# F1 of batch 0 kept in SBUF, with one f32 matmul a step, and its loads for F2 as two DMAs of four rows each

## The chip, the cores and the metric

The kernel runs on one core of one Trainium2 chip. The metric is the time of one execution on the device, in microseconds (us). Each kernel was timed in several runs; the profile is of one further execution. TensorE is called PE below, VectorE DVE, ScalarE ACT, GpSimd POOL, and SyncE, which issues all DMAs of this kernel, SP.

## What is computed

A spectral layer over 8 sequences (batches) of 3008 rows and 256 columns, and an MLP over all of its rows, in float32:

```python
X = np.fft.rfft(x, axis=1)
Yr = Xr @ w_r - Xi @ w_i + b_r
Yi = Xr @ w_i + Xi @ w_r + b_i
Yr = np.sign(Yr) * np.maximum(np.abs(Yr) - lam, 0.0)
Yi = np.sign(Yi) * np.maximum(np.abs(Yi) - lam, 0.0)
y = np.fft.irfft(Y, n=x.shape[1], axis=1)

h = y @ w_in
g = h - np.tanh(h)
return (g @ w_out).astype(np.float32)
```

w_in (256 x 2048) and w_out (2048 x 256) arrive as float64 and are taken apart on the chip into a high and a low float32 part.

## The kernel before

3008 = 64 x 47, and the Fourier transform is made in two factors. **F1** is the transform of length 47, over the rows of x; of its output 24 frequencies are needed, and real and imaginary parts of two of the 64 residues (a *pair*; there are 32) give 96 rows. **F2** is the transform of length 64, over the pairs. Each batch runs F1 (8 chunks of 4 pairs, class Forward), F2 with the linear layer and the shrinking (12 *units* of two frequencies each, class Spectrum), the inverse of F2 (still a unit; its result z goes to DRAM), and the inverse of F1 (class Unit, which reads z back). The MLP then takes chunks of 512 rows.

Between F1 and F2 the axis that lies on the partitions changes: F1 leaves 96 rows (parity, real or imaginary, frequency) by pair and column, and F2 needs 128 rows (parity, real or imaginary, pair) for one frequency. Before, batch 0 made that exchange in DRAM as the others do: `keep` copied a step's result from PSUM to a tile `st` and wrote it to `a_dram` (`a<-st`), and `load` of a unit read two frequencies back into the tile `at` (`at<-a`, one DMA of 256 KB).

All five engines run in an order that is written out by hand (`manual_schedule`), and each engine works through its own list in that order. Batch 0 stands at the start of the program:

- Loads on SP, in this order: the table of F1, the eight chunks `xt` of x, the table of F2. SP has one DMA queue.
- 11 matmuls on no data (`idle`) while the first loads come in.
- F1: 16 steps, two to a chunk. A step splits x into a high float32r part (a cast on ACT) and the rest (a subtraction on DVE), makes three matmuls of 512 columns (lines 235 to 237) and one idle matmul; two steps later `keep` (line 249) copies the result, on ACT or DVE. The loads of w_r, w_i, the biases and the table i1 are issued between the later steps.
- 16 idle matmuls.
- F2: in round i of a loop SP issues the load of unit i + 2, PE makes the transform of unit i (line 339), the products of unit i - 1 with the linear layer's weights (lines 442 and 448, which take the copies `xf` and the sum `sf` of the transform), and the inverse of unit i - 3 (line 471). The tile `at` has three buffers, so the load of unit i + 2 waits for the transform of unit i - 1. `combine_linear` (lines 125 to 139) and the split of i1 prepare the tables that the products and inverses need. Between these steps ACT and DVE take apart the first of the 16 pieces of w_in and w_out (`w_raw`, 512 KB each, loaded on the same queue; `some`).

In this stage F2 uses f32 matmuls, which the trace records as two matmuls each; an instruction's count in the trace is then twice that of the program.

Of the kernel before, what the change touches and what calls it, by code (L numbers as in the profile page):

```python
# [10 lines left out]
F32 = mybir.dt.float32  # L11
F32R = mybir.dt.float32r
# [5 lines left out]
NP, NJ = 32, 24  # L18
# [16 lines left out]
def dft_constants():  # L35
# [14 lines left out]
    di = np.stack([-s, c], 2).transpose(1, 0, 2, 3).reshape(128, 128)  # L50
    f2 = np.concatenate([dr[:, :96], dr[:, 32:], di[:, :96], -di[:, 32:]], 1)
    ph = 2 * np.pi * np.outer(np.arange(64), n1) / 64
    sg = np.where(np.arange(64) < 32, 1.0, -1.0)[:, None]
# [17 lines left out]
    i2 = i2.transpose(1, 0, 2).reshape(128, -1)  # L71
    return [np.ascontiguousarray(v, np.float32) for v in (f1, f1s, f2, i1, i2)]


@with_exitstack
def spectral_ffn(ctx, tc, x, w_r, w_i, b_r, b_i, w_in, w_out, x_twice, f1, f1s, f2, i1, i2, out):
    nc = tc.nc
# [62 lines left out]

    win_h = const.tile([P, 2, FF], F32R, name="win_h")
    win_l = const.tile([P, 2, FF], F32R, name="win_l")
    wout_h = const.tile([P, NF, D], F32R, name="wout_h")
    wout_l = const.tile([P, NF, D], F32R, name="wout_l")

# [26 lines left out]
    def split_f64(part, k, raw):  # L172
        if k < 2:
            sl = slice(part * WB, (part + 1) * WB)
            hi_out, lo_out = win_h[:, k, sl], win_l[:, k, sl]
        else:
            n = WB // D
            f = part * WB // P + (k - 2) * n
            hi_out, lo_out = (w[:, f:f + n].rearrange("p t e -> p (t e)") for w in (wout_h, wout_l))
        top, low = raw[:, :, 1], raw[:, :, 0]  # L180
# [28 lines left out]
    class Forward:  # L209
# [4 lines left out]
        def load(self):  # L214
            if self.ch == 0:
# [6 lines left out]
            nc.sync.dma_start(out=self.xt, in_=x[:, self.b * NP + self.ch * XC:self.b * NP + (self.ch + 1) * XC, :])  # L222
# [8 lines left out]
        def dft(self, q):  # L231
            xh, xl = self.x[q]
            self.ps[q] = bank("ps_f1")
            pv = self.ps[q][:96].rearrange("p (a d) -> p a d", d=D)
            nc.tensor.matmul(pv, f1l, xh, start=True, stop=False)
            nc.tensor.matmul(pv, f1h, xh, start=False, stop=False)
            nc.tensor.matmul(pv, f1h, xl, start=False, stop=True)

        def keep(self, q, copy=nc.scalar.copy):
            if self.b == 0 or self.b == 1 and self.ch >= LOOK:  # L240
                n = 2
                pool, tag, bufs = ((ffn, "th", 2), (work, "k", 5), (work, "tmp", 4))[(2 * self.ch + q) % 3] if self.b == 0 else (load, "at", 3)
                st = pool.tile([96, 2, D], F32, name="st", tag=tag, bufs=bufs)
            else:
# [67 lines left out]
    class Spectrum:  # L312
# [6 lines left out]
        def load(self):  # L319
            if self.jp == 0:  # L320
                z_dram[self.b] = dram.tile([NP, 96, D], F32, name=f"z_{self.b}", tag="z")
            self.at = load.tile([P, 2, D], F32, name="at", tag="at", bufs=3)
            nc.sync.dma_start(out=self.at.rearrange("p j d -> p (j d)"), in_=rows(a_dram[self.b][0], self.jp))
            if self.b > 2:
# [7 lines left out]
        def transform(self):  # L332
            ps = self.ps = bank("ps_f2")
            pv = ps.rearrange("p (t r j m) -> p t j r m", t=2, r=2, j=2)
            for jj in range(2):
                o = m0[2 * self.jp + jj]
                rhs = f2t.rearrange("p (r u c) -> p r u c", r=2, u=2)[:, :, :, o:o + 32]
                for t in range(2):
# [183 lines left out]
    class Chunk:  # L522
# [27 lines left out]
        def up(self, f, i):  # L550
            n = self.n
            hp = H[0][:, i % 2, :n] if H else early_h[i % 2 if i < SINGLE else 0][:, :n]
            k = 0
            for lhs, rhs in ((win_l, self.yh), (win_h, self.yh), (win_h, self.yl)):
                for t in range(2):
                    nc.tensor.matmul(hp, lhs[:, t, f * P:(f + 1) * P], rhs[:, t, :n], start=k == 0, stop=k == 5)  # L556
                    k += 1
# [10 lines left out]
        def down(self, f, gh, gl, t):  # L568
# [56 lines left out]
    class Pair:  # L625
# [13 lines left out]
        def left(self, name):  # L639
# [4 lines left out]
            t, f = {"a11": (0, 0), "a12": (1, 0), "a21": (0, 1), "a22": (1, 1)}[name]  # L644
            return [w[:, t, (2 * q + f) * P:(2 * q + f + 1) * P] for w in (win_h, win_l)]

# [51 lines left out]
    def weight_sums(p):  # L698
        wv = [w.rearrange("p k (q i m) -> p k i q m", i=2, m=P)[:, :, :, 2 * p:2 * p + 2] for w in (win_h, win_l)]
        pair = [work.tile([P, 2, 2, P], F32, name=f"ws{k}", tag="tmp", bufs=4) for k in range(2)]  # L700
# [233 lines left out]
    with tc.manual_schedule(engines={E.PE, E.Activation, E.DVE, E.Pool, E.SP}):  # L934
# [12 lines left out]
        nc.vector.memset(below, -LAM)
        f1h, f1l = split(load_whole(f1, [94, 96], "f1", tag="tmp", bufs=4), "f1", rest=nc.vector)
        first = [Forward(0, ch) for ch in range(NP // XC)]
        for f in first:  # L950
            f.load()
        f2t = load_const(f2, [P, 384], "f2")
        steps = [(f, q) for f in first for q in range(XC // 2)]
# [130 lines left out]
        for u in early_units[:3]:  # L1084
            for t in range(2):
                u.time(t)

        raw = work.tile([P, 2, 512], F32, name="raw", tag="raw", bufs=1)
        start.close()
# [149 lines left out]
```

## Time and profile before

| What | us |
|---|---|
| median of 3 runs | 2584.85 (2584.58 to 2585.59) |
| the profiled execution | 2586.71 |
| its span, from the first to the last instruction | 2584.9 |
| PE busy within the span | 2557.7 |

The profile is read in four views. The page gives busy times and shares. The chain follows the end of the program back to its start: at each step to what released it. The timeline lists instructions in order of time, with equal ones merged; the brackets at a row's end say how long the engine had stood idle and what ended it. The windows give, for a stretch of time, the busy time of each engine, the clock granted to PE as a share of the full one, and what the DMA engines did.

### The profile page before, as it was taken

The page shows a single profiled execution, that of the slowest core. Times are in us where ns is not written, and L with a number is a line of the kernel's source. Part 1 is how long each engine was busy: PE and PEld are TensorE (multiplying, and loading weights), DVE is VectorE, ACT ScalarE, POOL GpSimd, SP SyncE. Part 2 cuts the span into 40 slices and gives each one's busy share as a digit, 9 for nine tenths or more (in the row PEclk, how much of TensorE's full clock was granted, in tenths as well). Part 3 has the DMA queues.
Part 4 walks back from the last instruction along what each step waited for, and adds up shares of the span by engine and source line. Part 5 has one row for each costly group of instructions (what it writes and reads, how often), then busy time and mean ns, then how long its engine had stood idle before and what let it go on. Part 6 is the DMA issues. An engine that isn't in the chain of part 4 may idle for free.

```text
span 2584.9 us, 42892 instructions
## 1 busy us (share of the span) xinstructions
PE 2557.7 (99%) x16041; PEld 2283.9 (88%) x16041; DVE 1838.1 (71%) x2742; ACT 1608.0 (62%) x2942; POOL 792.4 (31%) x885
## 2 busy tenths in 40 slices
PE   8999999999999999999999999999999999999999
PEld 6787898899889999899999999899998999999998
DVE  6787884777777776777776777767777666666665
ACT  5556566666666666666666666666666555565655
POOL 0004334332334433333324333333333323221210
PEclk8999999999999999999999999999999999999999
DMA  6521225233333332333323342232433121111000
GB/s 192 169 84 56 89 72 152 82 99 97 95 105 118 104 116 82 98 112 107 120 72 115 97 132 90 86 116 84 131 91 95 62 73 60 47 43 47 19 27 17
DMA packets 145521, 235.87 MB, mean 91 GB/s; under 512 B 12192, under 2 KB 85152, under 8 KB 145312
## 3 DMA queue, kind: packets, MB, share of 16 engines
q1 hardware_dynamic: 145312, 233.11, 28.8%
q8 instruction: 127, 2.08, 0.3%
q14 instruction: 82, 0.67, 0.1%
HBM read 142.36 MB, written 90.70 MB: 90 GB/s over the span
## 4 chain that ended last, share of the span: by engine, by line
PE 95%; DVE 2%; DMA 1%; ACT 1%; issue 0%; POOL 0%; SPq 0%; DVEq 0%; ACTq 0%; POOLq 0%
PE o L580 39%; PE H L651 34%; PE ps_v L366 5%; PE ps_i L507 4%; PE ps_f L339 3%; PE ps_t L366 2%; PE he L556 2%; PE ps_f L285 1%; PE ps_v L448 1%; PE ps_i L413 1%; PE ps_i L415 1%; PE ps_i L414 1%; DMA a<-st 1%; PE oe L580 1%; PE ps_t L448 0%; PE ps_i L471 0%
## 5 line engine op out<-in xcount | busy, mean ns | idle before, releaser
L689 ACT CAST gh<-th 128x1024 fp32r<-128x1024 f32 x352 | 371.4, 1055 | 381.8 <-DVE th L685 253.5
L651 PEld LDWEIGHTS H<-y_t,sum 128*128 128x128 f32 x3168 | 516.2, 188 | 102.3 <-DVE th L685 5.5
L580 PE MATMUL o<-gh,wout_l 128*128 128x512 f32 x1408 | 563.2, 400 | 0.0
L580 PE MATMUL o<-gl,wout_h 128*128 128x512 f32 x1408 | 554.3, 394 | 0.5 <-DVE gl L693 0.5
L580 PE MATMUL o<-gh,wout_h 128*128 128x512 f32 x1408 | 552.7, 393 | 0.0
L651 PE MATMUL H<-y_t,sum 128*128 128x256 f32 x3168 | 545.2, 281 | 0.9 <-DVE ot L593 0.7
L693 DVE TENSOR_TENSOR gl<-th,gh 128x1024 fp32r<-128x1024 f32 x352 | 440.6, 1252 | 57.6 <-ACT gh L689 54.8
L685 DVE TENSOR_TENSOR th<-H,th 128x1024 f32<-128x1024 f32 x352 | 428.3, 1217 | 5.0 <-ACT th L682 2.3
L682 ACT ACTIVATE th<-H 128x1024 f32<-128x1024 f32 x352 | 362.6, 1030 | 42.5 <-PE H L651 42.0
L667 DVE TENSOR_TENSOR H<-H,late 128x256 f32<-128x256 f32 x352 | 152.2, 432 | 319.5 <-PE H L651 283.3
L580 PEld LDWEIGHTS o<-gl,wout_h 128*128 128x128 f32 x1408 | 264.7, 188 | 60.8 <-DVE gl L693 1.5
L673 DVE TENSOR_TENSOR H<-H,late 128x256 f32<-128x256 f32 x352 | 151.7, 431 | 191.4 <-PE H L651 183.1
L651 PE MATMUL H<-y_b,win_h 128*128 128x256 f32 x1408 | 280.8, 281 | 0.0
L580 PEld LDWEIGHTS o<-gh,wout_l 128*128 128x128 f32 x1408 | 265.0, 188 | 7.9 <-ACT gh L689 0.5
L580 PEld LDWEIGHTS o<-gh,wout_h 128*128 128x128 f32 x1408 | 264.9, 188 | 7.3
L659 ACT COPY late<-H 128x256 f32<-128x256 f32 x352 | 131.6, 374 | 211.9 <-PE H L651 209.1
L651 PE MATMUL H<-y_more,win_h 128*128 128x256 f32 x1408 | 263.1, 279 | 0.0
L97 POOL TENSOR_TENSOR z_l<-mn,z_h 128x512 fp32r<-128x512 f32 x84 | 112.5, 1340 | 431.3 <-ACT z_h L96 276.4
L651 PEld LDWEIGHTS H<-y_more,win_h 128*128 128x128 f32 x1408 | 215.3, 188 | 6.1
L651 PEld LDWEIGHTS H<-y_b,win_h 128*128 128x128 f32 x1408 | 214.4, 188 | 0.2 <-POOL y_b L97 0.2
L651 PE MATMUL H<-y_more,win_l 128*128 128x256 f32 x704 | 201.1, 286 | 1.2 <-DVE H L673 1.2
L403 DVE TENSOR_TENSOR y<-tb,ps_v 64x256 f32<-64x256 f32 x384 | 160.8, 419 | 56.8 <-PE ps_v L366 44.8
(190 smaller groups left out, 4381.3 us busy)
## 6 DMA issues: line engine op xcount, KB each, us to landing
a<-st SPq DMA_DIRECT2D x188, 192.0 KB, 3.0
x<-in_x_twice SPq DMA_DIRECT2D x55, 512.0 KB, 4.7
at<-a SPq DMA_DIRECT2D x96, 256.0 KB, 3.2
z<-zo SPq DMA_DIRECT2D x96, 256.0 KB, 2.0
zin<-z SPq DMA_DIRECT2D x64, 384.0 KB, 4.4
out<-ot SPq DMA_DIRECT2D x47, 512.0 KB, 3.1
shared<-a SPq DMA_DIRECT2D x60, 256.0 KB, 3.7
shared<-in_i SPq DMA_DIRECT2D x58, 235.0 KB, 4.0
```

Of the source, the lines that this page charges most:

```text
L97: rest.tensor_tensor(out=lo, in0=src, in1=hi.bitcast(F32), op=ALU.subtract)
L366: nc.tensor.matmul(dst, lhs[:, t], rhs[:, t, :], start=n == 0, stop=n == 5)
L403: nc.vector.tensor_tensor(out=y[ri * 64:(ri + 1) * 64, jj, :], in0=common(jj, ri), in1=self.vv[jj * 64:(jj + 1) * 64, ri * D:(ri + 1) * D] ...
L580: nc.tensor.matmul(self.o[t][:, :n], lhs[:, f, t * P:(t + 1) * P], rhs, start=f == 0 and k == 0, stop=f == NF - 1 and k == 2,)
L651: nc.tensor.matmul(dst, a, b, start=start and k == 0, stop=k == 2, skip_group_check=True)
L659: nc.scalar.copy(out=self.p7, in_=self.c11)
L667: nc.vector.tensor_tensor(out=self.c21, in0=self.acc, in1=self.p7, op=ALU.add)
L673: nc.vector.tensor_tensor(out=self.c22, in0=self.acc, in1=self.p7, op=ALU.add)
L682: nc.scalar.activation(out=self.th, in_=self.hp[:, :, :n], func=AF.Tanh)
L685: nc.vector.tensor_tensor(out=self.th, in0=self.hp[:, :, :self.n], in1=self.th, op=ALU.subtract)
L689: nc.scalar.copy(out=self.gh, in_=self.th)
L693: nc.vector.tensor_tensor(out=self.gl, in0=self.th, in1=h(self.gh), op=ALU.subtract)
```

## The change

F1 of batch 0 no longer splits x: a step is one f32 matmul on the loaded chunk. `keep` copies its result into one tile `first_a` in SBUF (96 rows; 32 KB in each), and nothing of it is written to DRAM. A unit's load is two DMAs from SBUF to SBUF, one for each of its two frequencies: each reads four rows of `first_a` (`first_a[row::NJ]`: rows `row`, `row` + 24, + 48, + 72), and spreads them, in pieces of 1 KB, over the 128 rows of `at`. The rows then come in another order, so batch 0 has its own table for F2 (`f2_first`), loaded in place of the old one; the old one is loaded after the first two units. 6 idle matmuls stand ahead of F1 instead of 11, and none between its steps. The loads for the linear layer are issued ahead of the steps.

To make room, the four tiles of the split w_in and w_out become two, for the lower and the upper half of the MLP's hidden columns; the second takes the place of `first_a` once F2 of batch 0 is over.

```diff
+    weights = [const.tile([P, 4, HF * D], F32R, name="weights0")]
+    first_a = work.tile([96, NP, D], F32, name="a_first", tag="weights1", bufs=1)
...
         def dft(self, q):
-            xh, xl = self.x[q]
             self.ps[q] = bank("ps_f1")
             pv = self.ps[q][:96].rearrange("p (a d) -> p a d", d=D)
+            if self.b == 0:
+                nc.tensor.matmul(pv, f1f, self.xt[:94, 2 * q:2 * q + 2], start=True, stop=True)
+                return
+            xh, xl = self.x[q]
...
         def keep(self, q, copy=nc.scalar.copy):
-            if self.b == 0 or self.b == 1 and self.ch >= LOOK:
+            if self.b == 0:
+                p = self.ch * XC + 2 * q
+                copy(out=first_a[:, p:p + 2], in_=self.ps[q][:96].rearrange("p (a d) -> p a d", d=D))
+                return
+            if self.b == 1 and self.ch >= LOOK:
...
             self.at = load.tile([P, 2, D], F32, name="at", tag="at", bufs=3)
+            if self.b == 0:
+                for jj in range(2):
+                    row = 2 * self.jp + jj
+                    nc.sync.dma_start(out=self.at[:, jj], in_=first_a[row::NJ])
+                return
...
-        idle(11)
+        idle(6)
...
-        for i in range(len(steps) + 2):
-            if 10 <= i < 14:
-                next(loads)
-            if i == 14:
-                i1f = load_whole(i1, [P, P], "i1", tag="s_l")
+        for _ in range(4):
+            next(loads)
+        i1f = load_whole(i1, [P, P], "i1", tag="s_l")
+        f1h, f1l = split(f1f, "f1", rest=nc.vector)
+        steps = [(f, q) for f in first for q in range(XC // 2)]
+        for i in range(len(steps) + 1):
             if i < len(steps):
-                steps[i][0].split(steps[i][1], piece(2 + i % 4, [94, 2, 2, D], F32R, "x_first"), nc.vector)
-            if 1 <= i <= len(steps):
-                steps[i - 1][0].dft(steps[i - 1][1])
-                idle(1)
-            if i >= 2:
-                f, q = steps[i - 2]
-                f.keep(q, nc.vector.tensor_copy if i % 3 == 0 else nc.scalar.copy)
+                steps[i][0].dft(steps[i][1])
+            if i >= 1:
+                f, q = steps[i - 1]
+                f.keep(q, nc.vector.tensor_copy if i % 2 == 0 else nc.scalar.copy)
...
         for u in units[:2]:
             u.load()
+        f2t = load_const(f2, [P, 384], "f2")
```

Two places show what that does to the lists. On SP, from the start of the program to the first loads for F2, before (`f_f` is F1's table, `f` F2's; `a` is the exchange in DRAM):

```order
L112 DMA f_f<-in_f 94x96
L222 DMA xt<-in_x 96x1024 x8
L107 DMA f_125<-in_f 128x384
L252 DMA a_108<-st 96x2x256 x8
L121 DMA bias<-in_b_r 128x256
...
L252 DMA a_108<-st 96x2x256 x4
L323 DMA at<-a_108 128x512 x2
L165 DMA w_raw<-in_moe_w_in 128x1024 x2
L323 DMA at<-a_108 128x512 x4
L421 DMA z_348<-zo 128x512
```

and now:

```order
L113 DMA f_f<-in_f 94x96
L229 DMA xt<-in_x 96x1024 x8
L113 DMA f_f<-in_f_first 128x384
L122 DMA bias<-in_b_r 128x256
...
L339 DMA at<-a_first 128x1x256 x4
L108 DMA f_203<-in_f 128x384
L173 DMA w_raw<-in_moe_w_in 128x1024 x2
L339 DMA at<-a_first 128x1x256 x8
L439 DMA z_196<-zo 128x512
```

The writes to DRAM are gone, each load is two, and the old table stands between the loads of unit 1 and the first two pieces of w_in.

On PE, from the start to unit 0 of F2, before (the second step's rows read as the first's, and so on to the last):

```order
L943 MATMUL idle<-warm 128x512 x11
L235 MATMUL ps_f_136<-x_first,f_l 96x512
L236 MATMUL ps_f_136<-x_first,f_h 96x512
L237 MATMUL ps_f_136<-x_first,f_h 96x512
L943 MATMUL idle<-warm 128x512
...
L943 MATMUL idle<-warm 128x512 x17
L339 MATMUL ps_f_375<-f_125,at 128x2x64 x4
```

and now:

```order
L962 MATMUL idle<-warm 128x512 x6
L242 MATMUL ps_f_128<-xt,f_f 96x512
...
L242 MATMUL ps_f_172<-xt,f_f 96x512
L962 MATMUL idle<-warm 128x512 x16
L357 MATMUL ps_f_228<-f_f,at 128x2x64 x4
```

Four matmuls a step have become one. Behind unit 0's transform PE, ACT, DVE, POOL and SP have the same operations in the same order as before, save for the doubled loads and the tiles' names.

More of the change, by code (lines that the diff above doesn't have):

```diff
@@ L51, in dft_constants @@
     f2 = np.concatenate([dr[:, :96], dr[:, 32:], di[:, :96], -di[:, 32:]], 1)
+    f2b = f2.reshape(NP, 4, 384).transpose(1, 0, 2).reshape(128, 384)
     ph = 2 * np.pi * np.outer(np.arange(64), n1) / 64
@@ L71, in dft_constants, with spectral_ffn @@
     i2 = i2.transpose(1, 0, 2).reshape(128, -1)
-    return [np.ascontiguousarray(v, np.float32) for v in (f1, f1s, f2, i1, i2)]
+    return [np.ascontiguousarray(v, np.float32) for v in (f1, f1s, f2, f2b, i1, i2)]
 @with_exitstack
-def spectral_ffn(ctx, tc, x, w_r, w_i, b_r, b_i, w_in, w_out, x_twice, f1, f1s, f2, i1, i2, out):
+def spectral_ffn(ctx, tc, x, w_r, w_i, b_r, b_i, w_in, w_out, x_twice, f1, f1s, f2, f2_first, i1, i2, out):
     nc = tc.nc
@@ L139, in combine_linear, with w_up, w_down @@
         return (wr, w2, w3), (ones, brow)
[L141 to L144, printed above, removed]
+    HF = NF // 2
+    weights = [const.tile([P, 4, HF * D], F32R, name="weights0")]
+    first_a = work.tile([96, NP, D], F32, name="a_first", tag="weights1", bufs=1)
+    def w_up(t, f, n=1):
+        lo = t * HF * P + f % HF * P
+        return [weights[f // HF][:, v, lo:lo + n * P] for v in range(2)]
+    def w_down(f, lo, n):
+        lo += f % HF * D
+        return [weights[f // HF][:, 2 + v, lo:lo + n] for v in range(2)]
     shared, turns = [], {}
@@ L173, in split_f64 @@
         if k < 2:
-            sl = slice(part * WB, (part + 1) * WB)
-            hi_out, lo_out = win_h[:, k, sl], win_l[:, k, sl]
+            hi_out, lo_out = w_up(k, part * WB // P, WB // P)
         else:
@@ L178, in split_f64 @@
             f = part * WB // P + (k - 2) * n
-            hi_out, lo_out = (w[:, f:f + n].rearrange("p t e -> p (t e)") for w in (wout_h, wout_l))
+            hi_out, lo_out = w_down(f, 0, WB)
         top, low = raw[:, :, 1], raw[:, :, 0]
@@ L214, in load @@
         def load(self):
-            if self.ch == 0:
+            if self.ch == 0 and self.b > 0:
                 a_dram[self.b] = dram.tile([2, NP, 96, D], F32, name=f"a_{self.b}", tag="a")
@@ L553, in up @@
             k = 0
-            for lhs, rhs in ((win_l, self.yh), (win_h, self.yh), (win_h, self.yl)):
+            for v, rhs in ((1, self.yh), (0, self.yh), (0, self.yl)):
                 for t in range(2):
-                    nc.tensor.matmul(hp, lhs[:, t, f * P:(f + 1) * P], rhs[:, t, :n], start=k == 0, stop=k == 5)
+                    nc.tensor.matmul(hp, w_up(t, f)[v], rhs[:, t, :n], start=k == 0, stop=k == 5)
                     k += 1
@@ L644, in left @@
             t, f = {"a11": (0, 0), "a12": (1, 0), "a21": (0, 1), "a22": (1, 1)}[name]
-            return [w[:, t, (2 * q + f) * P:(2 * q + f + 1) * P] for w in (win_h, win_l)]
+            return w_up(t, 2 * q + f)
         def product(self, dst, left, right, start=False):
@@ L698, in weight_sums @@
     def weight_sums(p):
-        wv = [w.rearrange("p k (q i m) -> p k i q m", i=2, m=P)[:, :, :, 2 * p:2 * p + 2] for w in (win_h, win_l)]
+        wv = [weights[p // 2][:, v].rearrange("p (k q i m) -> p k i q m", k=2, i=2, m=P)[:, :, :, 2 * (p % 2):2 * (p % 2) + 2] for v in range(2)]
         pair = [work.tile([P, 2, 2, P], F32, name=f"ws{k}", tag="tmp", bufs=4) for k in range(2)]
@@ L951, in spectral_ffn @@
             f.load()
-        f2t = load_const(f2, [P, 384], "f2")
-        steps = [(f, q) for f in first for q in range(XC // 2)]
+        f2b = load_whole(f2_first, [P, 384], "f2", tag="spill", bufs=1)
         loads = linear_loads()
@@ L1086, in spectral_ffn @@
                 u.time(t)
+        weights.append(work.tile([P, 4, HF * D], F32R, name="weights1", tag="weights1", bufs=1))
         raw = work.tile([P, 2, 512], F32, name="raw", tag="raw", bufs=1)
```

14 lines of the change are left out of this document (7 added, 7 removed).

## The prediction

> **What bounds the kernel now.** The page comes first: span, busy shares, and the chain of work that ended last, by engine.
>
> ```profile
> span 2584.9 us, 42892 instructions
> ...
> PE 2557.7 (99%) x16041; PEld 2283.9 (88%) x16041; DVE 1838.1 (71%) x2742; ACT 1608.0 (62%) x2942; POOL 792.4 (31%) x885
> ...
> PE 95%; DVE 2%; DMA 1%; ACT 1%; issue 0%; POOL 0%; SPq 0%; DVEq 0%; ACTq 0%; POOLq 0%
> ```
>
> TensorE (PE) ends everything: it is busy 99% of the span. What is to be had lies in the few stretches in which PE waits or works at a lower clock. The change touches only F1 and F2 of batch 0, so the second view is the chain in order of time over the first 60 us (start, length, what).
>
> ```profile
> 1.55 4.71 DMA xt<-in_x
> ...
> 7.49 8.67 DMA a<-st
> ...
> 20.55 5.22 DMA a<-st
> ...
> 26.49 3.92 DMA a<-st
> ...
> 30.55 2.72 DMA at<-a
> ...
> 33.40 3.76 PE ps_f L339 x16
> ```
>
> Until 33.40 the chain is transfers: x comes in, F1's results go out to DRAM (a<-st, three long pieces), and come back (at<-a). Only from 33.40, when F2 starts, is it PE. The third view is PE's timeline (start, length, engine, line, operation, idle time before with its releaser).
>
> ```profile
> 1.91 4.23 PE L943 MATMUL idle<-warm 128*128 128x512 f32 x11 [1.91 <-DVE below L947]
> ...
> 25.57 4.05 PE L943 MATMUL idle<-warm 128*128 128x512 f32 x17
> ...
> 33.40 3.76 PE L339 MATMUL ps_f<-f,at 128*128 128x128 f32 x16 [3.78 <-DMA at<-a]
> ...
> 42.84 1.06 PE L339 MATMUL ps_f<-f,at 128*128 128x128 f32 x8
> ...
> 46.95 1.05 PE L339 MATMUL ps_f<-f,at 128*128 128x128 f32 x8
> ...
> 51.06 1.02 PE L471 MATMUL ps_i<-mn,i_f 128*128 128x512 f32 x2
> 51.91 1.05 PE L339 MATMUL ps_f<-f,at 128*128 128x128 f32 x8
> 52.90 0.49 PE L442 MATMUL ps_v<-brow,ones 33*128 33x512 f32 x1
> ...
> 86.64 1.05 PE L339 MATMUL ps_f<-f,at 128*128 128x128 f32 x8
> ```
>
> L339 is a unit's transform in F2. Units 0 and 1 start at 33.40, unit 2 at 42.84, unit 3 at 46.95, unit 4 at 51.91, unit 11 at 86.64: from unit 3 on one unit takes (86.64 - 46.95) / 8 = 4.96 us. The last view, by windows, says who sets that, and at which clock (length, busy us of each engine, granted clock, DMA share, GB/s).
>
> ```profile
> 15.00:20.00 5.00, 2.60 (x8) 1.52 (x9) 2.60 (x5) 3.77 (x8) 0.00 (x0) 0.87 0.79 258
> 14.70:17.30 2.60, 0.00 (x0) 0.00 (x0) 0.00 (x0) 1.07 (x3) 0.00 (x0) 1.00 1.09 381
> 18.70:22.10 3.40, 3.40 (x10) 2.20 (x9) 3.04 (x5) 1.93 (x5) 0.00 (x0) 0.50 0.49 144
> ...
> 32.40:42.50 10.10, 9.10 (x28) 7.57 (x29) 2.97 (x7) 1.69 (x3) 0.00 (x0) 0.50 0.66 220
> ...
> 51.91:86.64 34.73, 34.73 (x163) 26.67 (x161) 27.47 (x59) 21.76 (x41) 0.00 (x0) 1.00 0.62 213
> ```
>
> From 51.91 to 86.64 PE is never idle at the full clock, so the 4.96 us are PE's own. From 32.40 to 42.50, after the idle 3.78 us, it runs at clock 0.50; likewise from 18.70 to 22.10, after the idle 14.70 to 17.30. The program's order after F2's start is the same before and after. So **the sum is how much earlier unit 3 starts than 46.95**; behind it PE carries on back to back, if the loads keep up.
>
> **The change part by part.** *F1.* Removed: 16 casts on ScalarE and 16 subtractions on VectorE, three matmuls a step, and 16 idle matmuls. Added: one f32 matmul a step, straight from x. L471 is such a matmul of 512 columns: two records, 51.91 - 51.06 = 0.85 us. So 16 x 0.85 = 13.6 us. It can begin when the first x is there.
>
> ```profile
> L222 SPq DMA_DIRECT2D xt<-in_x x8: 334/426/428, 1.2 to 4.3; - x8
> ...
> DMA to landing us min/median/max: 3.7/7.3/10.2
> ```
>
> The first x lands at 1.2 + 3.7 = 4.9, the last at 4.3 + 10.2 = 14.5, about one in 1.4 us, while two steps take 1.7: PE, not x, sets the pace, and F1 would end at 4.9 + 13.6 = 18.5. The 11 first idle matmuls took 0.38 us each, the 17 later ones 0.24, so PE begins slowly; with six of them instead of eleven it may still be at half clock when x comes. If that lasts one stretch of 3.4 us (as 18.70 to 22.10 did), it costs 1.7, and F1 ends at 20.2. I take the middle, **19.4**. The copies out of PSUM hide behind PE: one a step, on two engines in turn.
>
> ```profile
> L249 ACT COPY st<-ps_f 96x512 f32<-96x512 f32 x11 | 6.4, 583 | 6.3 <-DMA a<-st 4.1 <-PE ps_f L237 2.2
> L249 DVE COPY st<-ps_f 96x512 f32<-96x512 f32 x5 | 3.4, 680 | 0.0
> ```
>
> Only the last shows: 0.68 on VectorE, and some 0.2 of handing over, then the first load is issued at **20.3** (before: 30.55). The 16 writes a<-st with their waits are gone. What VectorE prepares for the linear part stands behind that copy:
>
> ```profile
> 27.68 0.69 DVE L128 SCALAR_TENSOR_TENSOR w_f<-wr_f,wi_f 128x512 f32<-128x512 f32 x1 [2.29 <-DMA wr_f<-in_w_r]
> ...
> 31.20 0.29 DVE L97 TENSOR_TENSOR i_l<-i_f,i_h 128x128 fp32r<-128x128 f32 x1
> ```
>
> From 27.68 to 31.49, 3.8 us; it now runs beside the first loads and is done by 24.1, before its first user (29.1, below).
>
> *F2's loads* are the unknown. Before: one DMA of 256 KB a unit from DRAM, 128 rows on both sides. Now: two DMAs of 128 KB, from four SBUF rows of 32 KB, in pieces of 1 KB.
>
> ```profile
> at<-a SPq DMA_DIRECT2D x96, 256.0 KB, 3.2
> z<-zo SPq DMA_DIRECT2D x96, 256.0 KB, 2.0
> ...
> w_raw<-in_moe_w_in SPq DMA_DIRECT2D x8, 512.0 KB, 5.3
> w_raw<-in_moe_w_out SPq DMA_DIRECT2D x8, 512.0 KB, 5.8
> ...
> i<-in_i SPq DMA_DIRECT2D x2, 705.0 KB, 4.5
> ...
> f<-in_f SPq DMA_DIRECT2D x1, 192.0 KB, 10.8
> ```
>
> First the rate of one DMA engine: in 15.00:20.00, when a<-st ran in pieces of 1 KB, 258 GB/s came from 0.79 of 16 engines, 20.4 GB/s each, or 50 ns a piece. The first at<-a took 2.72 us; 16 KB on each of 16 engines is 0.8 of it, so 1.9 is latency. Then the spread. No DMA of the trace has fewer than 48 rows on a side, so none shows four. Bounds: over 16 engines as the 128 rows of at<-a, 8 pieces each, 0.4 us a DMA; one source row an engine, 32 pieces, **1.6 us** a DMA, and both DMAs of a unit behind one another on the same four. I take four: four rows is what the source has to deal out, and the queue, one for all, gives the second DMA no other place. The Trainium skill, "DMA: Bandwidth & Descriptors", section "Why a DMA increments its semaphore by 16 and not by 1", has a rule for it: the engines used are the largest number up to 16 that divides the slowest dimension of both patterns. Here (4 and 128) that is four, against the 16 that the nearest row would suggest. No run shows it yet; by the row instead of the rule the gain would be 14.5 us (first rival).
>
> With four: unit 0 lands at 20.3 + 1.9 + 2 x 1.6 = 25.4, unit 1 at 28.6. Behind them on the same queue stand the second table (192 KB: 0.6) and two w_raw (512 KB: 1.6 each), then unit 2: 28.6 + 3.8 + 3.2 = 35.6; unit 3 at 38.8. PE's idle matmuls end at 19.4 + 3.8 = 23.2; unit 1's transform is done at 28.6 + 0.5 (half of 52.90 - 51.91) = 29.1. Unit 0's products take 46.95 - 42.84 - 0.99 = 3.1 us at full clock, 6.2 at half. Between 23.2 and 29.1 PE works 2.0 of 5.9 us, less than from 15 to 20 (2.60 of 5.00), where the clock fell, so I expect a half-clock spell; 29.1 + 6.2 = 35.3 still lies under the wait for unit 2 at 35.6. Only what lasts longer shows; I add 0.3. The skill's "TensorE: Matmul & The Clock Gate", section "Part 1: The HAM clock gate", lowers the clock after a whole idle window of about 3.4 us; by that there'd be no spell, and 0.3 less. The trace disagrees: 2.6 idle us (14.70:17.30) were enough.
>
> Unit 2's transform ends at 36.1, unit 1's products 3.1 later: **unit 3 starts at 39.2 + 0.3 = 39.5, 7.4 us earlier.**
>
> *Steady state.* Each of the four engines has, a unit, 3.2 for the loads and 256 KB / 16 / 20.4 = 0.8 for z; over the eight units also four w_raw (6.4) and two i (2.2 each), 1.35 a unit: 5.35 against 4.96, 3.1 us too much in all. Before, a load was issued 8 us ahead of its use:
>
> ```profile
> 52.78 0.32 SPq L421 DMA_DIRECT2D z<-zo  x1
> 53.15 0.43 SPq L169 DMA_DIRECT2D w_raw<-in_moe_w_out  x1
> 53.69 0.44 SPq L323 DMA_DIRECT2D at<-a  x1
> 57.73 0.32 SPq L421 DMA_DIRECT2D z<-zo  x1
> ```
>
> This one (53.69) is for unit 6, which starts at 51.91 + 2 x 4.96 = 61.83: 8.1 us, of which 1.9 + 3.2 are needed. The 3.0 left just about cover the 3.1. I put it at nothing; uncovered, it costs 0 to 3. The second issue a unit (0.44 on SP) is hidden: SP stands idle from 54.13 to 57.73. The weights' new tiles keep every operation and its order; nothing.
>
> **Sum.** The profiled execution took 2586.71 around its span of 2584.9, 0.07% over the median of 2584.85; the difference applies to either. 2584.85 - 7.4 = **2577.5**.
>
> **The rivals.** *Sixteen engines.* The loads land as at<-a did: units 0 and 1 by 20.3 + 1.9 + 1.6 = 23.8, close to the end of the idle matmuls at 23.2, and PE stays at full clock: two transforms (2.0), products (3.1), transform (1.0), products (3.1) put unit 3 at 32.4 to 33: 14.5 us earlier, **2570.4**. For it: every row of the trace has 16; against: none has four rows.
>
> *The one queue backs up.* The four engines' 3.1 us too much are not covered, SP takes longer to issue the regrouping loads than the 0.32 to 0.44 us of its rows, or the clock stays at half to the third unit as from 32.40 to 42.50 (2 us). Together 2.5 to 7: **2580 to 2585**.
>
> *Slow rows: slower than before.* Reading 32 pieces one after another out of a single partition may be slower than 50 ns. If a piece costs what 2 KB cost at that rate, 100 ns, each unit's loads hold four engines 6.4 us, with the rest 8.55 against PE's 4.96: eight units lose 28.7, the first three units 3.2 x 3 = 9.6. 38 lost against 7.4 won: about **2616**. It decides from about 60 ns a piece (1.9 lost at the start, 8 x 1.03 less 2.4 of cover after). For it: no row reads one partition for long; against: a<-st takes each of its pieces from one partition too.
>
> *It doesn't do what it says:* F1 could be held by x after all. Only its last two steps (1.7) hang on the last x, which lands at 14.5, so this could not put F1's end past 18.5.
>
> **How the numbers follow.** Forecast 0.52 (2575 to 2579.6), sixteen engines 0.20, backing up 0.18, slow rows 0.10 (0.03 of it near no change). A measurement of this kernel tells about 0.2%, 5.2 us, from no change: faster 0.72, same 0.18 + 0.03 = 0.21, slower 0.07. The range goes from sixteen engines with F1 at its earliest (2569.5) to most of the backing up (2583), and leaves out some 0.19.
>
> **What would show it.** Right: the f32 matmuls of F1 back to back from about 4.9 to 18.5 to 20.2; the first load issued near 20.3; at<-a_first landing in 3 to 9 us, the second of a pair 1.6 behind the first; PE waiting for it ahead of units 0, 1 and 2; unit 3 near 39.5, then 4.96 us a unit. Wrong: landings of 2 to 3 us (sixteen); units further apart than 4.96 with PE waiting for at<-a_first (backing up, slow rows); F1's matmuls with gaps.

## The result, and the profile after the change

The change made the kernel slower. The changed kernel takes 2605.53 us, the median of six runs (2588.87 to 2606.43), the kernel before 2585.28 beside it (2584.58 to 2585.89): a ratio of 1.0068, interval 1.0048 to 1.0089. The forecast was 2577.5. The profiled execution took 2605.9; these are the page's span, busy times and shares of the chain:

```profile
span 2604.1 us, 42744 instructions
...
PE 2580.2 (99%) x16004; PEld 2288.2 (88%) x16004; DVE 1828.7 (70%) x2729; ACT 1598.9 (61%) x2923; POOL 791.8 (30%) x885
...
PE 96%; DVE 2%; ACT 1%; DMA 1%; issue 0%; POOL 0%; SPq 0%; DVEq 0%; ACTq 0%; POOLq 0%
```

PE has 37 instructions fewer and is busy 22.5 us longer (2580.2 against 2557.7). So no new wait explains the loss: PE's own work got slower. PE's timeline says where it begins:

```profile
1.91 2.92 PE L962 MATMUL idle<-warm 128*128 128x512 f32 x6 [1.91 <-DVE below L966]
5.34 27.59 PE L242 MATMUL ps_f<-xt,f_f 94*96 94x512 f32 x32 [0.51 <-DMA xt<-in_x]
31.95 5.36 PE L962 MATMUL idle<-warm 128*128 128x512 f32 x16
...
38.40 0.71 PE L357 MATMUL ps_f<-f_f,at 128*128 128x128 f32 x4 [0.62 <-DMA at<-a_first]
40.10 0.68 PE L357 MATMUL ps_f<-f_f,at 128*128 128x128 f32 x4 [0.99 <-DMA at<-a_first]
42.03 1.23 PE L357 MATMUL ps_f<-f_f,at 128*128 128x128 f32 x4 [1.25 <-DMA at<-a_first]
...
48.59 1.05 PE L357 MATMUL ps_f<-f_f,at 128*128 128x128 f32 x8
...
52.69 1.06 PE L357 MATMUL ps_f<-f_f,at 128*128 128x128 f32 x8
...
57.65 1.05 PE L357 MATMUL ps_f<-f_f,at 128*128 128x128 f32 x8
```

F1 starts at 5.34 (4.9 was forecast) and has no gap, but its 32 records take 27.59 us, 0.86 each. The forecast had 0.43. That is half clock from the first to the last; F1 ends at 32.93. (The column of the granted clock has no record before 34.31; there the pace is the clock's witness.) The rest of the start went as forecast, only later. SP's timeline has the first loads, and the windows the clock behind them (length, busy us of each engine, granted clock, DMA share, GB/s):

```profile
33.74 3.35 SPq L339 DMA_DIRECT2D at<-a_first  x4
```

```profile
119.65:123.06 3.41, 3.41 (x13) 3.41 (x14) 2.13 (x6) 0.99 (x3) 0.00 (x0) 0.50 0.99 324
34.31:41.14 6.83, 4.87 (x25) 3.66 (x24) 2.23 (x6) 0.59 (x1) 0.00 (x0) 1.00 0.44 135
41.14:47.97 6.83, 5.94 (x15) 4.47 (x16) 2.37 (x6) 1.10 (x2) 0.00 (x0) 0.50 0.49 176
```

While nothing but at<-a_first moves, another window shows how many of the 16 DMA engines work, 0.27 of them or 4.3, at 96 GB/s:

```profile
35.50:38.40 2.90, 2.28 (x13) 1.66 (x12) 0.75 (x2) 0.00 (x0) 0.00 (x0) 1.00 0.27 96
```

Unit 3 starts at 52.69, 5.7 us later than before instead of 7.4 earlier. Then a unit takes 4.96 us, as before (57.65 - 52.69), up to unit 11, the last, whose two halves wait for their loads:

```profile
92.85 0.68 PE L357 MATMUL ps_f<-f_f,at 128*128 128x128 f32 x4 [0.32 <-DMA at<-a_first]
93.98 0.71 PE L357 MATMUL ps_f<-f_f,at 128*128 128x128 f32 x4 [0.45 <-DMA at<-a_first]
```

Without a wait the first would start at 87.41 + 4.96 = 92.37 and the second 0.5 us behind it.

The second half of the loss lies where no operation was changed. An MLP chunk casts its operand y_t once, on ACT; the view by tile gives the first and the last of the 44 (count, shortest, median and longest in ns, first and last start). Before:

```profile
L96 ACT CAST y_t<-raw x44: 400/408/412, 264.1 to 2531.9; 128x256 fp32r<-128x256 f32 x44
```

After:

```profile
L97 ACT CAST y_t<-raw x44: 400/408/412, 273.0 to 2550.4; 128x256 fp32r<-128x256 f32 x44
```

From the first to the last it was 2267.8 us, now it is 2277.4: **9.6 us lost evenly over the MLP.** One window of 2100 us shows how, before:

```profile
420.00:2520.00 2100.00, 2099.45 (x13622) 1902.48 (x13622) 1486.50 (x2145) 1327.93 (x2420) 691.70 (x773) 1.00 0.29 89
```

and after:

```profile
420.00:2520.00 2100.00, 2099.72 (x13558) 1899.55 (x13557) 1479.31 (x2138) 1326.35 (x2418) 695.52 (x777) 1.00 0.29 90
```

PE is never idle and at full clock in both, yet gets 64 matmuls less done; at 2100 / 13622 = 0.154 us each that is 9.9 us. The sum of the 19.2 us between the spans: 5.7 up to unit 3; 3.2 more up to the first y_t (273.0 - 264.1 = 8.9), of which unit 11's loads are one part (1.3) and a stretch at half clock from 119.65 another (above; 1.7); 9.6 in the MLP; 0.7 behind it.

### The profile page after: what moved, and what is told of

Same layout as the page of the kernel before. It is cut to its first block, busy times and chain, and to the rows that moved or that the text cites. A ratio compares the mean times of both kernels' runs of the same rounds, so it can differ in the third digit from the quotient of the medians.

```text
span 2604.1 us, 42744 instructions
## 1 busy us (share of the span) xinstructions
PE 2580.2 (99%) x16004; PEld 2288.2 (88%) x16004; DVE 1828.7 (70%) x2729; ACT 1598.9 (61%) x2923; POOL 791.8 (30%) x885
## 4 chain that ended last, share of the span: by engine, by line
PE 96%; DVE 2%; ACT 1%; DMA 1%; issue 0%; POOL 0%; SPq 0%; DVEq 0%; ACTq 0%; POOLq 0%
PE o L599 39%; PE H L670 33%; PE ps_v L384 5%; PE ps_i L525 4%; PE ps_f L357 3%; PE ps_t L384 2%; PE he L574 2%; PE ps_f L298 1%; PE ps_f L242 1%; PE ps_v L466 1%; PE ps_i L432 1%; PE ps_i L433 1%; PE ps_i L431 1%; PE oe L599 1%; DMA at<-a_first 1%; PE ps_i L489 0%
## 5 line engine op out<-in xcount | busy, mean ns | idle before, releaser
L599 PE MATMUL o<-gh,weights 128*128 128x512 f32 x2816 | 892.2, 398 | 0.0
L599 PE MATMUL o<-gl,weights 128*128 128x512 f32 x1408 | 555.1, 394 | 0.5 <-DVE gl L712 0.5
L599 PEld LDWEIGHTS o<-gh,weights 128*128 128x128 f32 x2816 | 443.1, 188 | 16.2 <-ACT gh L708 0.5
L670 PE MATMUL H<-y_b,weights 128*128 128x256 f32 x2112 | 364.3, 281 | 0.0
L599 PEld LDWEIGHTS o<-gl,weights 128*128 128x128 f32 x1408 | 264.5, 188 | 63.3 <-DVE gl L712 1.4
L670 PE MATMUL H<-y_more,weights 128*128 128x256 f32 x2112 | 310.8, 283 | 1.2 <-DVE H L692 1.2
L670 PEld LDWEIGHTS H<-y_b,weights 128*128 128x128 f32 x2112 | 298.9, 188 | 0.1
L670 PEld LDWEIGHTS H<-y_more,weights 128*128 128x128 f32 x2112 | 284.4, 189 | 16.2 <-DVE H L692 1.9
L293 POOL TENSOR_TENSOR x<-x,x 64x512 fp32r<-64x512 f32 x55 | 71.2, 1294 | 258.2 <-issue 133.1
L679 ACT COPY H<-H 128x256 f32<-128x256 f32 x352 | 125.7, 357 | 11.2
```

Of the source, the lines that this page charges most:

```text
L599: nc.tensor.matmul(self.o[t][:, :n], lhs, rhs, start=f == 0 and k == 0, stop=f == NF - 1 and k == 2,)
L670: nc.tensor.matmul(dst, a, b, start=start and k == 0, stop=k == 2, skip_group_check=True)
```

## The experiments

Two causes were to be told apart from their rivals: F1's clock (theory 1 in the expectations), and something that slows all of the MLP, of which the new places of the tiles in SBUF were the first suspect (theory 2). Each run's time stands beside runs of the kernel before on the same chip (2585 to 2586 us in all). "e9" and the like are the runs' short names.

### F1's clock

**e1: 11 idle matmuls ahead of F1, as before the change, instead of 6.**

```diff
-        idle(6)
+        idle(11)
```

> The changed kernel with 11 idle matmuls ahead of F1 instead of 6, as before the change. Theory 1 (too few idle matmuls leave PE at half clock when F1 begins, and F1's f32 matmuls of 94x96 do not raise it): the clock is at full from 5 to 8 us on, an F1 record takes 0.43 us instead of 0.86, F1 ends near 20 instead of 32.9, the first load is issued near 21 instead of 33.7, total about 2605.5 - 13 = 2592.5. If F1's matmuls do not even hold a clock once granted, F1 falls back after one or two windows of 3.4 us: end near 26 to 29, total 2596 to 2601. Rival (F1's clock is hidden, the loads on four engines or the new places of the tiles cost the 20 us): within 3 of 2605.5.

2592.86 us (2590.87 to 2594.34), ratio 1.0025 (1.0016 to 1.0035): 12.7 less than the changed kernel. PE's timeline:

```profile
1.91 5.06 PE L962 MATMUL idle<-warm 128*128 128x512 f32 x11 [1.91 <-DVE below L966]
6.77 14.36 PE L242 MATMUL ps_f<-xt,f_f 94*96 94x512 f32 x32
...
40.21 1.05 PE L357 MATMUL ps_f<-f_f,at 128*128 128x128 f32 x8
```

F1 takes 14.36 us instead of 27.59, and unit 3 starts at 40.21. The time is that of theory 1 (2592.5): a full clock, once granted, is kept through F1's 14 us, but F1 by itself does not win it. The one run of the changed kernel at 2588.87 fits a clock that 6 idle matmuls (2.9 us) leave to chance; it was not profiled, so that is not shown for this run.

**Why does F1 not raise the clock? e2 pads its table to 128 columns, e8 its contraction to 128 rows, e16 lets 94 rows do the idle matmuls.** e2 and e8 are the changed kernel with 6 idle matmuls, e16 is e9 (below) with 11.

```diff
e2:
+                nc.tensor.matmul(pv, f1p, ...)      # f1p: [94, 128], columns 96 to 127 zero
e8:
+                nc.tensor.matmul(pv, f1p, self.xt[:, 2 * q:2 * q + 2], start=True, stop=True)   # 128 rows, the last zero
e16:
-                nc.tensor.matmul(ps, warm[:, :P], warm, start=True, stop=True)
+                nc.tensor.matmul(ps, warm[:rows, :P], warm[:rows], start=True, stop=True)       # rows = 94 for the first 11
```

> The changed kernel with F1's table padded with 32 columns of zeros (94x128 stationary, 128 rows of PSUM written, 96 kept), 6 idle matmuls. If the share of the array in use decides whether the clock is raised: full clock within two windows of 3.4 us after F1's start, an F1 record goes from 0.86 to 0.43 us, F1 ends at 19 to 24, total 2592 to 2597. If the columns do not matter (f32, or 94 rows, is what keeps the clock low): 0.86 us a record throughout, F1 ends near 32.9, total near 2605.5.

> The changed kernel (6 idle matmuls) with F1's contraction padded from 94 to 128 rows by zeros in the table and in x (128x96 stationary). If the rows in use decide whether the clock is raised: full clock within two windows of 3.4 us of F1's start, 0.43 us a record, F1's end at 19 to 24 instead of 32.9. If neither rows nor columns decide (f32 at 512 columns, say): 0.86 us a record to the end, as with the columns padded. The run may by chance start at full clock.

> The same kernel (2581.3) with the 11 first idle matmuls on 94 rows instead of 128, float32r as they are. If the rows in use decide whether the clock is raised: they do not raise it, F1 runs at half clock to its end (0.86 us a record, 27.6 us in all), and the time is 2581.3 + 13 = 2594. If it is F1's f32 that cannot raise it, and float32r can whatever its rows: full clock by 8 us as with 128 rows, 2581 within 3.

One execution each: e2 2607.9 us, e8 2595.48, e16 2595.39. F1's row in e2:

```profile
5.52 27.65 PE L243 MATMUL ps_f<-xt,f_f 94*128 94x512 f32 x32 [0.67 <-DMA xt<-in_x]
```

F1 in e8, and e8's windows:

```profile
6.99 15.64 PE L244 MATMUL ps_f<-xt,f_f 128*96 128x512 f32 x32 [2.04 <-DMA xt<-in_x]
```

```profile
7.00:10.40 3.40, 3.40 (x6) 1.33 (x7) 0.94 (x2) 0.61 (x2) 1.29 (x3) 0.69 1.03 267
10.40:13.80 3.40, 3.40 (x7) 1.10 (x6) 0.69 (x1) 1.15 (x2) 0.00 (x0) 0.81 1.04 269
13.80:17.20 3.40, 3.40 (x9) 1.30 (x8) 1.37 (x2) 1.13 (x3) 0.00 (x0) 1.00 1.05 271
```

PE's timeline in e16:

```profile
1.91 5.06 PE L963 MATMUL idle<-warm 94*128 94x512 f32 x11 [1.91 <-DVE below L966]
6.77 27.51 PE L243 MATMUL ps_f<-xt,f_f 94*96 94x512 f32 x32
```

More columns change nothing. In e8 the clock is full when F1 begins (0.69 of the first 3.40 us is 1.3 us at full clock, the rest at half): the six idle matmuls, 2.92 us as in the changed kernel, have raised it here and not there, so six do leave it to chance. It then falls to half, behind the wait of 2.04 us, and with 128 rows comes back within F1 (0.69, 0.81, 1.00), with the same f32 matmuls of 512 columns. And 11 float32r matmuls on 94 rows (5.06 us) do not raise it, where 11 on 128 rows do (e1). So it is the rows that the matmul uses: 94 of 128 keep a full clock but did not raise a half one. Each of the three is one execution, and no run has a number of rows between 94 and 128.

### What slows the MLP

**e3: the kernel before, with nothing but the weights' new inner order. e4: the changed kernel with weights and tables at their old places. e5: e4 with 11 idle matmuls.**

```diff
e3 (kernel before):
+    weights = [const.tile([P, 4, HF * D], F32R, name=f"weights{k}") for k in range(2)]   # and w_up, w_down
e4 (changed kernel):
+    win = [const.tile([P, 2, FF], F32R, name=f"win_{'hl'[v]}") for v in range(2)]
+    first_a = const.tile([96, NP, D], F32, name="a_first", tag="wout", bufs=1)
...
+        wout.append(const.tile([P, 2, NF * D], F32R, name="wout", tag="wout", bufs=1))
```

> The kernel before, with nothing changed but the two tiles weights0 and weights1 (lower and upper half of the hidden columns, high and low part together) in the same 64 KB of each partition in which the four tiles of w_in and w_out stood. Theory 2 (where the weights stand lengthens PE's matmuls by a few ns each through the whole MLP): 2585.3 + 8 to 10 = 2593 to 2595, growing evenly from 270 us to the end; o<-gl behind o<-gh 2 to 3 ns further apart. Rival (the weights' inner order is nothing; the drift comes with the other tiles that moved, or with the later start): 2585.3 within 1.5.

> The changed kernel with the weights where they stood before the change: win_h, win_l, and one tile for both parts of w_out, at their old addresses; F1's result lies in w_out's place until F2 of batch 0 is over; the constants (the linear layer's tables) are back at their old places too, while xh, ot, st and the shared tables stay where the change put them. 6 idle matmuls. Theory 2: the even drift of 10 us from 270 us to the end goes, total about 2595. Rival (the moved work tiles or the later start make the drift): 2605.5 within 2. If part comes from each: in between.

> The changed kernel with both: 11 idle matmuls ahead of F1, and the weights and the linear layer's tables where they stood before the change. If the two causes are separate, their gains add: 2605.5 less 13 for F1's clock less 13 for the places (2591.8 of the run with 6 idle matmuls came with F1 at half clock in its profile) gives 2579, and all runs lie within a few us, since with 11 idle matmuls F1's clock is no longer left to chance. If one hides the other: 2588 or more.

e3: 2586.62, ratio 0.9998 (0.9989 to 1.0006). The inner order is nothing, against theory 2. e4: 2591.81 (2578.38 to 2599.15), in two groups, five of its twelve times under 2584, as with a clock left to chance; the profiled one at 2592.04 has F1 at half clock, 27.59 us. Its 44 chunks take 2265.0 us, the drift is gone. e5: 2582.49 (2579.25 to 2584.06), ratio 0.9984 (0.9975 to 0.9993). The two causes nearly add up (12.7 and 13.7 us less than the changed kernel alone, 23.0 together), and with both put right the change is a small gain. What remained was which place matters.

**e6: w_out's tile, the tables and at go back to the change's places. e7: the tables lie ahead of all weights, which move up by 18 KB.** Both are otherwise as e5.

```diff
e6:
+    first_a = work.tile([96, NP, D], F32, name="a_first", tag="wout", bufs=1)
e7:
+    for name, shape, dtype in (("bias", [P, 2, D], F32), ("f1_h", [94, 96], F32R), ...):
+        pre[name] = const.tile(shape, dtype, name=name)     # ahead of win
```

> As the version with both, but the one tile of w_out lies where the change put weights1 (from 58272 bytes on in a partition), and with it the linear layer's tables and the three tiles at go down to where the change has them (33920 to 58272); win_h and win_l stay. Theory 2a (the drift comes from one of these: the outer 32 KB of the weights, the tables, or at): 2579 + 10 to 13 = 2589 to 2592, growing evenly from 270 us. Theory 2b (it needs the change's halves, high and low part of w_in and w_out in one tile, beside the moved place): 2579 within 2.

> As the version with both, but the linear layer's tables and F2's stand ahead of all weights, which move up by 18 KB, in one piece; at stays at 84896. If the tables' low place or any shift of the weights makes the drift: 2579 + 10 = 2589. If it is at's place, or the gap between the two halves of the weights: 2579 within 2.

e6: 2589.7, ratio 1.0015 (1.0006 to 1.0024), 7.2 more than e5: part of the drift is back. (Its profiled execution was its fastest, 2586.8; there the chunks take 2272.5 us against 2268.5 in e5.) e7: 2580.3, ratio 0.9977 (0.9968 to 0.9986): none (2265.9). So moving the weights does no harm by itself. The programs' addresses, which no view shows but which follow from the order and the sizes of the tiles, gave the next theory: in e6 w_out begins at byte 58272 of a partition, which is 32 past a multiple of 64, as weights1 does in the changed kernel. The cause would be a tile of one float, `below`, that takes 32 bytes and now stands ahead of weights1; in e7 and before, all weights begin at multiples of 128.

**e9 puts those 32 bytes behind weights1. e10 puts them ahead of the weights in the kernel before.**

```diff
e9 (changed kernel, 11 idle matmuls):
-        below = const.tile([P, 1], F32, name="below")
+    below = work.tile([P, 1], F32, name="below", bufs=1)      # right behind first_a
e10 (kernel before):
+    below = const.tile([P, 1], F32, name="below")
     win_h = const.tile([P, 2, FF], F32R, name="win_h")
```

> The changed kernel with 11 idle matmuls, and one tile of 32 bytes (below) allocated behind weights1 instead of ahead of it. The tile weights1, the tables and at thereby lie 32 bytes lower, at multiples of 64 (58240 instead of 58272 for weights1); all else stays, the halves and the far place too. Theory 2c (the drift comes from weights whose rows begin 32 bytes past a multiple of 64): no drift from 270 us on, 2593 less 10 = 2582 to 2584. Rival (the place, 58 KB instead of 34 KB, whatever the 32 bytes): 2590 to 2593.

> The kernel before, with that tile of 32 bytes allocated ahead of the weights instead of behind them: all four weights tiles 32 bytes higher (1184 instead of 1152, and so on), nothing else moved and no instruction changed. Theory 2c: the change put half of the weights off and lost 10 us over the MLP; with all of them off about twice that, 2586 + 14 to 22 = 2600 to 2608. Rival: 2586 within 1.5.

e9: 2581.3 (2579.59 to 2584.2), ratio 0.9984 (0.9975 to 0.9993); its chunks take 2268.5 us against 2277.0 in e1. e10: 2605.18, ratio 1.0077 (1.0062 to 1.0093). e10 is the cleanest run of all: no instruction differs from the kernel before, only the weights lie 32 bytes higher, and 19 us are lost. Its chunks:

```profile
L96 ACT CAST y_t<-raw x44: 400/408/412, 261.7 to 2546.7; 128x256 fp32r<-128x256 f32 x44
```

2285.0 us against 2267.8. In the MLP only PE reads the weights, so it is taken to be PE's reading that slows.

**But multiples of what? e11 and e12 put every tile at a multiple of 64, e13 the weights 64 past one of 128, e14 all that PE reads at multiples of 128.** e11 and e14 are the changed kernel with 11 idle matmuls, e12 and e13 the kernel before.

```diff
e11, e12:
+        scalars = const.tile([P, 16], F32, name="below")      # below and rebias in one tile of 64 bytes
+        below, rebias = scalars[:, 0:1], scalars[:, 1:2]
e13: the same, ahead of win_h
e14:
+        scalars = ffn.tile([P, 16], F32, name="below", bufs=1)   # behind gl and gh
```

> The changed kernel with 11 idle matmuls and the two tiles of 32 bytes (below, rebias) made one of 64, so that every tile begins at a multiple of 64; in all kernels so far the MLP's moving operands of the first products (the y tiles and sums) begin 32 bytes past one. If only the stationary side counts: as the run with weights1 alone put right, 2582 to 2584. If the moving side counts as well: 2572 to 2581.

> The kernel before with the two tiles of 32 bytes made one of 64: the weights stay where they are (multiples of 64 already), the tables, the y tiles and the sums come to multiples of 64. If only the stationary side counts, and the linear layer's tables are too few to tell: 2586 within 2. If the moving side counts: 2576 to 2584.

> The kernel before with the one tile of 64 bytes ahead of the weights: all weights tiles begin 64 bytes past a multiple of 128 (1216, 17600, ...), all else as in the kernel before with every tile at multiples of 64 (2585.7). If multiples of 128 are what the weights need: 2586 + 14 to 22 = 2600 to 2608, as with 32 bytes. If multiples of 64 do: 2586 within 2, and the drift of the changed kernel with all tiles at multiples of 64 needs another cause.

> The changed kernel with 11 idle matmuls and the two small tiles made one of 64 bytes behind gl and gh, so that every tile that PE reads begins at a multiple of 128. If only the large weights matter: 2581 within 2, as with weights1 alone put right. If the sums, xh and xl, s and zin, which stand for the stationary side in a third of the MLP's first products and in the units, gain as the weights do (3 ns for each of some 5000 matmuls): 2566 to 2577.

e11: 2596.2, ratio 1.0043 (1.0026 to 1.0060). e12: 2585.7, 0.9995 (0.9986 to 1.0005). e13: 2598.39, 1.0047 (1.0032 to 1.0062). e14: 2602.34, 1.0069 (1.0049 to 1.0089). Neither e11 nor e14 came near either of its expectations. Alignment as such is refuted: e14, with everything at multiples of 128, is nearly as slow as the changed kernel, although its F1 runs at full clock (13.90 us). The chunks in e14:

```profile
L97 ACT CAST y_t<-raw x44: 401/409/413, 257.7 to 2546.3; 128x256 fp32r<-128x256 f32 x44
```

Side by side, with the places of what PE holds (weights, sums) and of what it streams past them (y, gh, gl) as bytes past a multiple of 128, a pattern shows. The 44 chunks are last less first y_t; the other columns are the mean time from one matmul's start to the next one's, in ns, from the trace's records between 300 and 2560 us (starts more than 400 ns apart left out).

| run | weights | sums | y | gh, gl | 44 chunks, us | weights x y_b | weights x y_more | weights x gh | sums x y_t |
|---|---|---|---|---|---|---|---|---|---|
| before | 0 | 32 | 32 | 64 | 2267.8 | 117.6 | 119.0 | 234.0 | 117.9 |
| e10 | 32 | 32 | 32 | 64 | 2285.0 | 120.0 | 121.2 | 237.8 | 118.5 |
| e13 | 64 | 64 | 64 | 64 | 2278.9 | 118.9 | 120.8 | 237.0 | 118.5 |
| e14 | 0 | 0 | 0 | 0 | 2288.6 | 118.9 | 120.7 | 237.1 | 120.2 |
| e12 | 0 | 64 | 64 | 64 | 2265.7 | 116.3 | 117.9 | 234.0 | 119.8 |

For the products with the weights: held and streamed operand begin in opposite halves of 128 bytes, 116.3, 117.9, 234.0 (e12); in the same half, 118.9, 120.7, 237.1 (e14). With y at 32 they lie in between (before), with weights and y at 32 they are worst (e10). A rule of one pair alone does not cover all: weights at 32 against gh at 64 take the longest, 237.8 (e10), and the sums, at the same places as y_t, take 119.8 in e12 and 118.5 in e13, where the weights lie elsewhere. So what stands beside a matmul counts too. In e12 the products with the weights gain what those with the sums, now in the same half as y, lose.

**e17 and e18: held operands at 0, streamed ones at 64, in the changed kernel (11 idle matmuls) and in the one before.**

```diff
+    for k in range(6):
+        work.tile([P, 1024], F32, name="place", tag=f"sum{k}", bufs=1)
+    scalars = work.tile([P, 16], F32, name="below", bufs=1)     # what follows begins 64 past
+    below, rebias = scalars[:, 0:1], scalars[:, 1:2]
```

> The changed kernel with 11 idle matmuls and the tiles placed so that what PE loads as weights in the MLP (the weights, the sums) begins at a multiple of 128 bytes and what it streams against them (the y tiles, gh, gl) begins 64 bytes past one. Theory 2d (a matmul's stream and the weight load beside it slow each other by some 3 ns when both begin in the same half of 128 bytes, or when one begins 32 past a multiple of 64 and lies over both): all pairs at their fastest at once; against the run with weights1 put right (2581.3) the products with the sums go from 118.6 ns to about 116.5, the others of the first products from 119.0 and 116.9 to 117.9 and 116.3: 8 to 10 us less, 2571 to 2574. Rival (each tile's own place counts, multiples of 128 are good for some and bad for others): no less than 2580.

> The kernel before with the same places (weights and sums at multiples of 128, y tiles 64 past one, gh and gl 64 past as before), no instruction changed. Theory 2d: the products with the sums from 117.9 ns to 116.5, the others from 117.6 and 119.0 to 116.3 and 117.9: 3106 x 1.4 + 2073 x 1.3 + 2070 x 1.1 ns = 9 us less than 2586, 2575 to 2579. Rival: 2584 or more.

e17: 2571.56 (2569.93 to 2578.26), ratio 0.9956 (0.9942 to 0.9969). e18: 2575.73 (2574.27 to 2578.26), ratio 0.9966 (0.9954 to 0.9979). Both are as theory 2d has it, and **e17 beats both kernels**. e17's chunks and window:

```profile
L97 ACT CAST y_t<-raw x44: 402/408/413, 258.6 to 2516.7; 128x256 fp32r<-128x256 f32 x44
```

```profile
420.00:2520.00 2100.00, 2099.27 (x13674) 1897.99 (x13673) 1491.31 (x2152) 1331.31 (x2430) 695.75 (x779) 1.00 0.29 89
```

2258.1 us, and 52 matmuls more than before in the same window. Pair by pair the theory did less well than in the sum: weights x y_b came to 115.5 ns (116.3 expected), sums x y_t to 117.1 (116.5), weights x y_more to 118.6 (117.9); shared x zin came to 118.8 against 121.0 before, but it is 118.9 in the slow e10 and e1 too.

### The loads

**e15: e9, with the second load of each unit issued by ACT on its own queue.**

```diff
-                    nc.sync.dma_start(out=self.at[:, jj], in_=first_a[row::NJ])
+                    (nc.sync, nc.scalar)[jj].dma_start(out=self.at[:, jj], in_=first_a[row::NJ])
```

> The changed kernel with 11 idle matmuls and weights1 at a multiple of 128 (2581.3), and the second of a unit's two loads issued by ScalarE on its own queue. If the queue decides which four engines a DMA of four rows gets: both land together, about issue + 3.3 instead of + 4.6, unit 1 at issue + 5 instead of + 8.2, and the third unit starts up to 3 us earlier: 2577 to 2580. If the second DMA has the same four engines: no landing moves by more than the 0.6 us that SP no longer spends on its issue, 2580 to 2582.

2588.23 (2584.39 to 2590.32), ratio 1.0006 (0.9997 to 1.0015): 7 us worse than e9, which neither expectation had. The transforms of units 0 and 1 in e9:

```profile
25.41 0.68 PE L358 MATMUL ps_f<-f_f,at 128*128 128x128 f32 x4 [0.47 <-DMA at<-a_first]
26.68 0.71 PE L358 MATMUL ps_f<-f_f,at 128*128 128x128 f32 x4 [0.59 <-DMA at<-a_first]
28.18 0.91 PE L358 MATMUL ps_f<-f_f,at 128*128 128x128 f32 x4 [0.80 <-DMA at<-a_first]
29.82 1.22 PE L358 MATMUL ps_f<-f_f,at 128*128 128x128 f32 x4 [0.73 <-DMA at<-a_first]
```

and in e15:

```profile
27.14 1.13 PE L358 MATMUL ps_f<-f_f,at 128*128 128x128 f32 x8 [2.36 <-issue]
29.38 1.19 PE L358 MATMUL ps_f<-f_f,at 128*128 128x128 f32 x4 [1.11 <-DVE sf L456]
31.82 1.23 PE L358 MATMUL ps_f<-f_f,at 128*128 128x128 f32 x4 [1.25 <-DMA at<-a_first]
```

In e9 four halves come one by one. In e15 unit 0's two are there together, half a microsecond after the second of e9, and unit 1 is 2 us later. The windows show the engines. In this one the trace's packets are pieces of a_first alone, about as many on either queue:

```profile
34.10:36.00 1.90, 1.90 (x6) 1.45 (x6) 1.90 (x6) 0.09 (x1) 0.00 (x0) 0.50 0.27 96
```

It is the share and the rate of the one queue in the changed kernel (0.27, 96): the second queue puts no further engine to work. That the four are the same ones is the plain reading; no view names a DMA's engines. What follows on SP's queue now runs beside the second load. Unit 3 starts at 42.80, 2.5 us later than in e9; the rest of the loss comes in later units, most of it ahead of unit 8:

```profile
71.27 1.13 PE L358 MATMUL ps_f<-f_f,at 128*128 128x128 f32 x8 [3.49 <-DMA at<-a_first]
```

ACT issues its loads between its own operations; whether that, or the order on the queues, makes these late was not tested apart.

## Why the prediction was wrong

- **F1.** The step that failed first is "if that lasts one stretch of 3.4 us ... it costs 1.7, and F1 ends at 20.2". The doubt was right, its size was not: half clock lasted through F1, 27.59 us from 5.34 on, and F1 ended 13.5 us later than the 19.4 taken. The step let any work of PE raise the clock; the changed kernel, e2 and e16 show that 94 rows did not, e8 that 128 did. The row it took its 3.4 us from (18.70 to 22.10) had an idle matmul on 128 rows in every four, and the change takes these out. The Trainium skill, "TensorE: Matmul & The Clock Gate", section "What's actually happening", has the clock rise after one busy window of about 3.4 us; here 27.6 us of back-to-back F1, at least seven such windows, did not raise it. 16 x 0.85 itself was right where the clock was full: 14.36 in e1, 13.96 in e7.
- **The end of F1 to the first load.** 0.8 us (32.93 to 33.74), against 0.9 forecast (19.4 to 20.3).
- **Loads on four engines.** Right: 0.27 of 16 engines (above), and a DMA of 128 KB takes 1.4 us at 96 GB/s (1.6 forecast). Counted from the first issue, unit 0's second half starts 4.7 after it (5.1 forecast), unit 1's 8.3 (8.3), unit 3 19.0 (19.2). The wait for unit 2 did not come: PE reached it 14.9 after the first issue without a gap, so its load (15.3 forecast) had landed, and PE's work at half clock set the start of unit 2. The rule of the Trainium skill's "DMA: Bandwidth & Descriptors", section "Why a DMA increments its semaphore by 16 and not by 1", that gave four agrees. With F1 at full clock unit 3 starts at 40.21 in e1; the forecast was 39.5.
- **The half-clock spell** came as expected (41.14 to 47.97, 0.50).
- **Steady units.** 4.96. The term put at nothing ("uncovered, it costs 0 to 3") is there: the four engines' backlog showed ahead of unit 11, whose transform ends 1.3 us late here and 1.8 late in e1.
- **"The weights' new tiles keep every operation and its order; nothing."** This step failed by 9.6 us. The first half of the sentence holds, e3 shows even that the new order of the weights is nothing. But the move of one tile of 32 bytes put half of the weights off their place against gh, gl and y. Nothing in the profile of before could give the size; the list of addresses could have raised the question.
- **The rivals.** None had either mechanism; "slower" was given 0.07, and to a rival (slow rows) that did not come.
- With both put right (e9) the change brings 5.1 us (2586.43 less 2581.3) of the 7.4. Some 3 us are lost between unit 3 and the first chunk: unit 3 is 6.7 earlier than before in e1, the first y_t 3.8 (260.3 against 264.1). Unit 11's loads take 1.8 of them; where the rest goes stays open.

## What to carry to other kernels

Where matmuls followed an idle start, ones on all 128 rows had to raise the clock first: the stage of 94 rows ran at the clock that it found, and too few idle matmuls ahead of it cost 13 us here. After any change to tiles, compare the addresses of the operands that PE reads in the long loops; 32 bytes ahead of them were worth 19 us, and the right places, held and streamed operand beginning in opposite halves of 128 bytes, 9 us without a changed instruction (e18). A loss or gain spread evenly over code that nobody touched is found by two landmarks far apart, not by the list of waits.

## What was not expected of the hardware

- Matmuls on 94 rows hold a full clock (14.36 us in e1) but did not raise it in 27.6 us; with zero rows added the clock came back within F1 (e8), with zero columns it did not rise (e2).
- The places of PE's two operands in a partition change the time of a float32r matmul by up to 4 ns in 117 and 4 in 234. The Trainium skill, "TensorE: Matmul & The Clock Gate", section "Step-by-step: what each phase is for", says that a weight load takes no read bandwidth from the running matmul, since PE has two read ports; these runs show that the time still depends on where both operands lie. That it is the load of the next weights beside the stream that collides is a reading; shown is only the dependence on the places. Nor is it settled why all at 0 (e14, 2288.6) is worse than all at 64 (e13, 2278.9).
- Two loads of four rows on two queues worked on 0.27 of the DMA engines, as on one (e15): 96 GB/s in all, and the second queue gained nothing.
